# Banded attention and mixture of experts on one core: exponentials and last sums kept in PSUM, scaling on ScalarE, weight blocks stored by the queue of loads

## The chip, the core and the metric

The kernel runs on one core of a Trainium2 chip. The metric is the device time of one execution in microseconds (us). The kernel before takes 1236.85 us, the median of three runs (1235.83 to 1238.42). TensorE is written PE (its weight loads PEld), VectorE is DVE, ScalarE is ACT, GpSimd is POOL, and SyncE, which here only issues transfers, is SP.

## The reference

There are four batches, each of 8 heads, 768 positions and head size 64. For every query the scores over the keys get a slope times distance as bias; only the first `n_global` (8) keys and the last `n_local` (96) keys up to the query itself are kept. Then comes a softmax and the product with v:

```
a = exp(scores - max(scores)); a = a / (sum(a) + 1e-9); attn = a @ v
x = attn with the heads side by side        # 3072 rows x 512
p = domain_probs / (domain_probs.sum(-1) + 1e-9)
for e in 4 experts:                          # w1: 512 x 1024, w2: 1024 x 512
    out += p[:, e] * (relu(x @ w1[e]) @ w2[e])
```

All inputs and outputs are fp32.

## The kernel before

**Order of the work.** The attention of batch 0 runs alone ("first attention"). Then each batch's mixture of experts runs with the attention of the next batch spread between its products; batch 3's mixture runs alone. Up to a point shortly after the first attention every engine follows the program's order (`Ordered.on`). After that a planner orders the instructions of each engine by its own costs, with the program's order as priority. Engines take their own instructions strictly in order.

**Attention.** A tile is 128 queries of two heads (a pair), so there are 24 tiles in a batch. `scores` writes the scores of both heads into one PSUM bank (`ps`). `softmax` works on two tiles at a time. For the newer tile DVE adds the bias, finds the extreme and writes the biased scores to an SBUF tile `pb` (this is the custom instruction in the profile), and ACT takes the exponential in place in `pb` and sums it into `zsum`. For the older tile DVE adds 1e-9 to `zsum`, takes the reciprocal and multiplies the two halves of `pb` by it. `turn` transposes `pb` through PE into a PSUM tile `pt`, which ACT copies to SBUF as `pT`, and `weigh` multiplies with v into `px`. The bank `ps` is free once the biased scores are in SBUF. The first attention has 3 `ps`, 4 `pt` and 1 `px` banks; the later ones have 2, 2 and 1, and 3 banks `pm` are left for the mixture.

**Mixture.** Each expert's hidden width is cut into four, so a batch has 16 units. A unit has two parts. `first` makes a quarter of x @ w1 by seven block products in the manner of Strassen and Winograd, each of them six matmuls of 384 columns into one `pm` bank: A11, S2, S1, S3, A12, S4, A22 in this order. Partial sums go through the SBUF tiles p1, u, vv and c22. The last four products finish one of the four blocks of the hidden layer each: DVE adds the product and a partial sum (`add`), ACT takes the relu into the upper part of h (`relu`), and DVE later forms the lower part of h as relu minus the upper part. That "late" instruction is put off to the next `add` or the next product of `second` (`work_late`). `second` makes six tiles of h @ w2, each six matmuls of 512 columns into one `pm` bank, which DVE multiplies by the expert's probability and adds to `acc`. The program runs first(i), second(i-1), first(i+1), and so on. The three `pm` banks are handed out in the order of the products, so a product needs the bank of the third product before it.

**Weights.** Every unit's blocks of w1 and w2 are built once, while batch 0 runs: SP loads the raw weights, POOL forms the block sums, ACT and POOL split them into two parts. `load_w1` and `load_w2` end with `keep`, a store of the finished block to DRAM issued from POOL. The later batches load the kept blocks through SP (`fetch`). There are two buffers for each of w1 and w2 blocks, so a unit's buffer is written again two units later.

All engine calls go through one helper, so nearly every instruction shows the line L42 in the profile, and the tiles' names tell them apart. In the trace the sums of the last four products are `c<-pm,vv`, `p<-pm,p`, `vv<-pm,vv` and `u<-pm,u`, the relus are ACT `h<-c`, `h<-p`, `h<-vv`, `h<-u`, and the late instructions are DVE `h<-c,h`, `h<-p,h`, `h<-vv,h`, `h<-u,h`.

Of the kernel before, what the change touches and what calls it, by code (L numbers as in the profile page):

```python
# [9 lines left out]
F32 = mybir.dt.float32  # L10
F32R = mybir.dt.float32r
# [7 lines left out]
P = 128  # L19
# [6 lines left out]
def f32(ap):  # L26
    return ap.bitcast(F32)
# [158 lines left out]
def attn_moe_kernel(ctx: ExitStack, tc, q, k, v, n_global, n_local, domain_probs, w1, w2, out):  # L186
# [88 lines left out]
    class Pools:  # L275


        def __init__(self, stack, name, st, kd, qd, nat, natv, pb, ps, pt):
            def sbuf(part, bufs):
                return stack.enter_context(tc.tile_pool(name=f"{name}_{part}", bufs=bufs))  # L280

            def psum(part, bufs):
                return stack.enter_context(tc.tile_pool(name=f"{name}_{part}", bufs=bufs, space=PSUM))

            self.st, self.natv = sbuf("st", st), sbuf("natv", natv)
            self.kd, self.qd, self.nat, self.vg = sbuf("kd", kd), sbuf("qd", qd), sbuf("nat", nat), sbuf("vg", kd)
            self.pb, self.pT, self.small = sbuf("pb", pb), sbuf("pT", 4), sbuf("small", pb)
            self.ps, self.pt, self.px = psum("ps", ps), psum("pt", pt), psum("px", 1)
# [113 lines left out]
    def softmax(A, new, old):  # L402


        if old:
            pb, zsum = old["pb"], old["zsum"]
        if new:
            t, pr, ps = new["t"], new["pr"], new["ps"]
            cols = slice(0, P) if t == 0 else slice(0, 2 * P)
            bcol = slice(2 * P, 3 * P) if t == 0 else slice(0, 2 * P)  # L410
            new["pcol"] = pcol = slice(P, 2 * P) if t == 0 else slice(0, 2 * P)
            nmax = A.small.tile([P, 2], F32, name="nmax")
            new["zsum"] = A.small.tile([P, 2], F32, name="zsum")
            new["pb"] = A.pb.tile([P, 2, 2 * P], F32, name="pb")
        for j in range(2):
            if new:
                ve.tensor_tensor_reduce(
                    new["pb"][:, j, pcol], ps[:, j, cols], nbias[:, 2 * pr + j, bcol],
                    1.0, 3.0e38, ALU.add, ALU.min, nmax[:, j : j + 1],
                )  # L420
                ac.activation(
                    new["pb"][:, j, pcol], new["pb"][:, j, pcol], AF.Exp, bias=nmax[:, j : j + 1], scale=-1.0,
                    accum_out=new["zsum"][:, j : j + 1],
                )
            if old:
                if j == 0:
                    ve.tensor_scalar_add(zsum, zsum, 1e-9)
                else:
                    ve.reciprocal(zsum, zsum)
        if old:  # L430
            for j in range(2):
                ve.tensor_scalar_mul(pb[:, j, old["pcol"]], pb[:, j, old["pcol"]], zsum[:, j : j + 1])

    def turn(A, tile_):

# [198 lines left out]


    dp = main.enter_context(tc.tile_pool(name="dp", bufs=1, space=bass.MemoryType.DRAM))
    kept = {}

    def keep(key, dst):
        kept[key] = dp.tile(list(dst.shape), F32R, name="kept_{}_{}_{}".format(*key))  # L640
        po.dma_start(f32(kept[key]), f32(dst))

    def fetch(name, key, shape, view):
        dst = wp.tile(shape, F32R, name=name)
# [3 lines left out]
    def load_w1(i, wait=0, lead=5, hold=2):  # L648


        if i >= len(units):
            return
        b, e, g = units[i]
        if b > 0:
            wts[(i, 1)] = fetch("w1s", (e, g, 1), [P, 2, 7, 2, P], lambda t: {
                name: t[:, :, n] for n, name in enumerate(("A11", "A12", "A22", "S1", "S2", "S3", "S4"))
            })
            return
        for _ in range(wait):
            yield 1  # L660
        raw = rp.tile([P, KT, 2 * P], F32, name="raw1")
        sy.dma_start(raw, w1[e, :, g * 2 * P : (g + 1) * 2 * P].rearrange("(a p) f -> p a f", p=P))
        for _ in range(lead):
            yield 1
        a11, a21 = raw[:, 0:2, :P], raw[:, 0:2, P:]
        a12, a22 = raw[:, 2:4, :P], raw[:, 2:4, P:]
        sums = rp.tile([P, 4, 2, P], F32, name="sums")
        s1, s2, s3, s4 = (sums[:, n] for n in range(4))
        po.tensor_add(s1, a21, a22)
        po.tensor_sub(s2, s1, a11)  # L670
        po.tensor_sub(s3, a11, a21)
        po.tensor_sub(s4, a12, s2)
        for _ in range(hold):
            yield 1
        dst = wp.tile([P, 2, 7, 2, P], F32R, name="w1s")
        wts[(i, 1)] = {name: dst[:, :, n] for n, name in enumerate(("A11", "A12", "A22", "S1", "S2", "S3", "S4"))}
        for sl, src in (
            (slice(0, 2), raw[:, :, :P].rearrange("p (n a) f -> p n a f", n=2)),
            (slice(2, 3), a22.rearrange("p (n a) f -> p n a f", n=1)),
            (slice(3, 5), sums[:, 0:2]),  # L680
            (slice(5, 7), sums[:, 2:4]),
        ):
            ac.copy(dst[:, 0, sl], src)
            po.tensor_tensor(dst[:, 1, sl], src, f32(dst[:, 0, sl]), op=ALU.subtract)
            yield 1
        keep((e, g, 1), dst)

    def load_w2(i, lead=7):

# [12 lines left out]
        for f in range(2):  # L702
            ac.copy(dst[:, 0, f], raw[:, f])
            po.tensor_tensor(dst[:, 1, f], raw[:, f], f32(dst[:, 0, f]), op=ALU.subtract)
            yield 1
        keep((e, g, 2), dst)

    hs = {}

# [20 lines left out]
    def first(i):  # L730
# [9 lines left out]
        def add(out, pm, other):  # L740
            ve.tensor_add(out, pm[:, :HALF], other)
            work_late()

        p1, u, vv, c22 = (up.tile([P, HALF], F32, name=n) for n in ("p1", "u", "vv", "c22"))
        pm = product(i, "A11", "B11")
        ac.copy(p1, pm[:, :HALF])
        yield
# [2 lines left out]
        add(vv, product(i, "S1", "T1"), u)  # L750
        yield
        pm = product(i, "S3", "T3")
        add(c22, pm, vv)
        add(u, pm, u)
        relu(1, 1, c22)
        yield
        add(p1, product(i, "A12", "B21"), p1)
        relu(0, 0, p1)
        yield
        add(vv, product(i, "S4", "B22"), vv)  # L760
        relu(0, 1, vv)
        yield
        add(u, product(i, "A22", "T4"), u)
        relu(1, 0, u)
        yield

    accs = {}
# [1 line left out]
    def second(i):  # L769

        b, e, g = units[i]
        w2s, h = wts[(i, 2)], hs[i]
        for t in range(NQT):
            pm = ps_mm.tile([P, 512], F32, name="pm")
# [28 lines left out]
    bp = main.enter_context(tc.tile_pool(name="bp", bufs=1))  # L803
    Ordered.on = True
    with ExitStack() as start_stack:
        A = Pools(start_stack, "start", st=1, kd=2, qd=1, nat=2, natv=3, pb=4, ps=3, pt=4)
        for n, _ in enumerate(attention(0, A, early=True)):
            if n == 9:
                chores += [load_w1(0, lead=2), load_w2(0, lead=3)]
            if n == 18:  # L810
                chores.append(load_w1(1, lead=2, hold=3))
            if n == 2 * NQT + 5:
                chores.append(blocks(0, (0,), po))
            work_chores()
        mix = mixture()
        next(mix)
# [2 lines left out]
    up = main.enter_context(tc.tile_pool(name="up", bufs=1))  # L819
    op = main.enter_context(tc.tile_pool(name="op", bufs=1))  # L820
    ps_mm = main.enter_context(tc.tile_pool(name="ps_mm", bufs=3, space=PSUM))
    A = Pools(main, "att", st=1, kd=1, qd=1, nat=1, natv=1, pb=2, ps=2, pt=2)

# [76 lines left out]
```

## Time and profile before

| | us |
|---|---|
| median of three runs | 1236.85 |
| the profiled execution, device time | 1238.11 |
| its span, first to last instruction | 1236.3 |
| PE busy / weight loads | 1184.1 / 1055.6 |
| DVE busy | 922.9 |
| ACT busy | 429.7 |
| POOL busy | 241.2 |
| mean granted TensorE clock, as a share of full speed | 0.989 |

An engine's busy time is a sum over stages of different kinds: the first attention (to about 82 us), batch 0's mixture with batch 1's attention and the building of the weights (to about 372 us), two like stages without the building (to about 668 and 967 us), and batch 3's mixture alone. A row of the trace gives the start in us, the duration in us, the engine, what it writes and reads, the shape, the count where like rows are merged, and in brackets the idle time before it with what ended it.

### The profile page before, as it was taken

How to read it: one execution, taken by the hardware profiler on the slowest of the kernel's cores; microseconds unless marked ns; L12 is line 12 of the kernel's file. 1: busy time of each engine (PE TensorE's matmuls, PEld its weight loads, DVE VectorE, ACT ScalarE, POOL GpSimd, SP SyncE). 2: the span in 40 equal slices, each digit the busy share in tenths (PEclk: the TensorE clock that was granted, in tenths of full speed). 3: DMA queues.
4: the chain of work that ended last, by engine and by line, in shares of the span. 5: the costliest groups of instructions: out<-in, count | busy, mean ns of one | idle time of the engine just before them, and what ended most of it. 6: DMA issues, size and time to landing. Idle time of an engine off the chain costs nothing.

```text
span 1236.3 us, 18009 instructions
## 1 busy us (share of the span) xinstructions
PE 1184.1 (96%) x6624; PEld 1055.6 (85%) x6624; DVE 922.9 (75%) x2018; ACT 429.7 (35%) x1044; POOL 241.2 (20%) x258
## 2 busy tenths in 40 slices
PE   6779999999999999999999999999999999999998
PEld 4558898888888898898987898899898899999996
DVE  6878989877868777777767776867776866666665
ACT  4764454545442333333323233333332211111110
POOL 5576657466541000000002000000000100000000
PEclk9989999999999999999999999999999999999999
DMA  6557868786856666576655765757554555555532
GB/s 160 156 158 249 286 212 278 239 282 230 295 183 210 228 197 207 189 228 194 222 169 176 263 195 193 232 166 248 191 170 179 181 213 187 188 187 187 187 128 88
DMA packets 122704, 251.39 MB, mean 203 GB/s; under 512 B 83184, under 2 KB 91376, under 8 KB 106224
## 3 DMA queue, kind: packets, MB, share of 16 engines
q1 hardware_dynamic: 114256, 197.73, 50.5%
q0 software_dynamic: 4608, 46.14, 9.2%
q10 hardware_dynamic: 3744, 6.30, 1.4%
q8 instruction: 54, 0.88, 0.3%
q14 instruction: 42, 0.34, 0.1%
HBM read 174.11 MB, written 52.43 MB: 183 GB/s over the span
## 4 chain that ended last, share of the span: by engine, by line
PE 81%; DVE 9%; DMA 5%; ACT 2%; issue 1%; SPq 1%; POOL 1%; ACTq 0%; DVEq 0%; POOLq 0%
PE pm L42 71%; DMA qd<-st_q 5%; PE pt L42 4%; PE px L42 3%; PE ps L42 3%; DVE pb L42 3%; DVE h L42 1%; SPq L42 1%; DVE x L42 1%; ACT pb L42 1%; DVE zsum L42 1%; DVE u L42 1%; DVE xT L42 0%; DVE acc L42 0%; DVE vv L42 0%
## 5 line engine op out<-in xcount | busy, mean ns | idle before, releaser
L42 PE MATMUL pm<-w2s,h 128*128 128x512 f32 x2304 | 558.5, 396 | 9.5 <-DVE acc L42 9.1
L42 PEld LDWEIGHTS pm<-w2s,h 128*128 128x128 f32 x2304 | 429.1, 189 | 101.3 <-DVE acc L42 12.3
L42 DVE SCALAR_TENSOR_TENSOR acc<-pm,prob,acc 128x512 f32<-128x512 f32 x360 | 267.4, 748 | 120.9 <-PE pm L42 119.1
L42 PE MATMUL pm<-xT,w1s 128*128 128x384 f32 x1536 | 298.4, 339 | 4.9 <-ACT xT L42 3.0
L42 PEld LDWEIGHTS pm<-xT,w1s 128*128 128x128 f32 x1536 | 268.3, 189 | 8.2 <-ACT xT L42 3.4
L42 PE MATMUL pm<-xB,w1s 128*128 128x384 f32 x1152 | 229.1, 340 | 2.2 <-DVE vv L42 1.3
L42 PEld LDWEIGHTS pm<-xB,w1s 128*128 128x128 f32 x1152 | 202.5, 189 | 8.1 <-DVE vv L42 1.6
L42 ACT ACTIVATE pb<-pb,nmax 128x256 f32<-128x256 f32 (+1 forms) x192 | 93.1, 486 | 121.3 <-DVE nmax L42 114.2
L42 POOL COPY vg<-v 32x768 f32<-32x768 f32 x16 | 13.3, 829 | 525.7 <-DMA v<-in_v_dram 515.2
L42 ACT COPY p<-pm 128x384 f32<-128x384 f32 x64 | 30.6, 477 | 214.0 <-PE pm L42 213.9
L42 DVE TENSOR_SCALAR pb<-pb,zsum 128x256 f32<-128x256 f32 (+1 forms) x192 | 84.9, 474 | 2.8
L42 DVE TENSOR_TENSOR u<-pm,p 128x384 f32<-128x384 f32 x64 | 35.6, 556 | 61.1 <-PE pm L42 57.5
L42 DVE CUSTOM_DVE_ANT_0 pb<-ps,nbias 128x256 f32<-128x256 f32 (+1 forms) x192 | 71.9, 395 | 10.9 <-PE ps L42 7.1
L42 ACT ACTIVATE h<-c 128x384 fp32r<-128x384 f32 x64 | 33.6, 525 | 131.8 <-DVE c L42 131.8
L42 ACT COPY pT<-pt 128x512 f32<-128x512 f32 (+1 forms) x96 | 52.2, 544 | 76.0 <-PE pt L42 75.7
L42 DVE TENSOR_TENSOR u<-pm,u 128x384 f32<-128x384 f32 x128 | 70.5, 551 | 3.3 <-PE pm L42 2.6
L42 PE MATMUL pt<-ident,pb 128*128 128x128 f32 x352 | 57.2, 280 | 13.6 <-DVE pb L42 13.0
L42 PEld LDWEIGHTS pt<-ident,pb 128*128 128x128 f32 x352 | 43.3, 143 | 22.6 <-DVE pb L42 6.3
L42 PE MATMUL ps<-kd,qd 128*128 128x256 f32 x288 | 48.6, 283 | 6.0 <-DMA qd<-st_q 6.0
L42 PEld LDWEIGHTS ps<-kd,qd 128*128 128x128 f32 x288 | 44.5, 188 | 11.2 <-issue 7.2
L42 DVE TENSOR_TENSOR c<-pm,vv 128x384 f32<-128x384 f32 x64 | 35.6, 556 | 22.4 <-PE pm L42 21.7
L42 DVE TENSOR_TENSOR vv<-pm,u 128x384 f32<-128x384 f32 x64 | 35.6, 556 | 21.7 <-PE pm L42 21.0
(89 smaller groups left out, 1117.6 us busy)
## 6 DMA issues: line engine op xcount, KB each, us to landing
w1s<-kept SPq DMA_DIRECT2D x48, 1792.0 KB, 7.4
w2s<-kept SPq DMA_DIRECT2D x48, 1024.0 KB, 5.0
kept<-w1s POOLq DMA_DIRECT2D x16, 1792.0 KB, 6.6
qd<-st_q SPq DMA_DIRECT2D x96, 192.0 KB, 6.2
raw<-in_moe_w_dram SPq DMA_DIRECT2D x32, 512.0 KB, 4.4
kept<-w2s POOLq DMA_DIRECT2D x16, 1024.0 KB, 6.6
v<-in_v_dram SPq DMA_DIRECT2D x16, 384.0 KB, 4.2
out_dram<-acc ACTq DMA_DIRECT2D x24, 256.0 KB, 3.0
```

What stands on the lines that cost most here:

```text
L42: ins = fn(*args, **kwargs)
```

## The change

Four things change. In the first attention the biased scores and the exponentials stay in the `ps` bank, and only the scaling by DVE writes `pb`; there are 4 `ps` and 3 `pt` banks in place of 3 and 4. In the later attentions the addition of 1e-9 to `zsum` and the two scalings of a tile go from DVE to ACT (`Copy` with a bias or a scale); the reciprocal stays on DVE. In `first`, the last sum of each of the last four products is written back into the product's own `pm` bank, and relu and late instruction read it there; c22 is gone, and u takes the S3 product before c22's sum overwrites it. The stores of the built blocks are issued from SP at the beginning of the unit's `first` (w1) or `second` (w2).

```diff
-        def __init__(self, stack, name, st, kd, qd, nat, natv, pb, ps, pt):
+        def __init__(self, stack, name, st, kd, qd, nat, natv, pb, ps, pt, early):
+            self.early = early
...
+                e = new.setdefault("exp", {})[j] = ps[:, j, cols] if A.early else new["pb"][:, j, pcol]
                 ve.tensor_tensor_reduce(
-                    new["pb"][:, j, pcol], ps[:, j, cols], nbias[:, 2 * pr + j, bcol],
-                    1.0, 3.0e38, ALU.add, ALU.min, nmax[:, j : j + 1],
+                    e, ps[:, j, cols], nbias[:, 2 * pr + j, bcol], 1.0, 3.0e38, ALU.add, ALU.min, nmax[:, j : j + 1]
                 )
                 ac.activation(
-                    new["pb"][:, j, pcol], new["pb"][:, j, pcol], AF.Exp, bias=nmax[:, j : j + 1], scale=-1.0,
-                    accum_out=new["zsum"][:, j : j + 1],
+                    e, e, AF.Exp, bias=nmax[:, j : j + 1], scale=-1.0, accum_out=new["zsum"][:, j : j + 1]
                 )
             if old:
-                if j == 0:
+                if j == 1:
+                    ve.reciprocal(zsum, zsum)
+                elif A.early:
                     ve.tensor_scalar_add(zsum, zsum, 1e-9)
                 else:
-                    ve.reciprocal(zsum, zsum)
+                    ac.activation(zsum, zsum, AF.Copy, bias=1e-9)
         if old:
             for j in range(2):
-                ve.tensor_scalar_mul(pb[:, j, old["pcol"]], pb[:, j, old["pcol"]], zsum[:, j : j + 1])
+                if A.early:
+                    ve.tensor_scalar_mul(pb[:, j, old["pcol"]], old["exp"][j], zsum[:, j : j + 1])
+                else:
+                    ac.activation(pb[:, j, old["pcol"]], old["exp"][j], AF.Copy, scale=zsum[:, j : j + 1])
...
-    def keep(key, dst):
-        kept[key] = dp.tile(list(dst.shape), F32R, name="kept_{}_{}_{}".format(*key))
-        po.dma_start(f32(kept[key]), f32(dst))
+    def keep(i, n):
+        if (i, n) in waiting:
+            key, dst = waiting.pop((i, n))
+            kept[key] = dp.tile(list(dst.shape), F32R, name="kept_{}_{}_{}".format(*key))
+            sy.dma_start(f32(kept[key]), f32(dst))
...
-        keep((e, g, 1), dst)
+        waiting[(i, 1)] = (e, g, 1), dst
...
-        keep((e, g, 2), dst)
+        waiting[(i, 2)] = (e, g, 2), dst
...
-        p1, u, vv, c22 = (up.tile([P, HALF], F32, name=n) for n in ("p1", "u", "vv", "c22"))
+        def last(pm, other):
+            add(pm[:, :HALF], pm, other)
+            return pm[:, :HALF]
+
+        p1, u, vv = (up.tile([P, HALF], F32, name=n) for n in ("p1", "u", "vv"))
+        keep(i, 1)
...
         pm = product(i, "S3", "T3")
-        add(c22, pm, vv)
         add(u, pm, u)
-        relu(1, 1, c22)
+        relu(1, 1, last(pm, vv))
         yield
-        add(p1, product(i, "A12", "B21"), p1)
-        relu(0, 0, p1)
+        relu(0, 0, last(product(i, "A12", "B21"), p1))
         yield
-        add(vv, product(i, "S4", "B22"), vv)
-        relu(0, 1, vv)
+        relu(0, 1, last(product(i, "S4", "B22"), vv))
         yield
-        add(u, product(i, "A22", "T4"), u)
-        relu(1, 0, u)
+        relu(1, 0, last(product(i, "A22", "T4"), u))
...
         b, e, g = units[i]
+        keep(i, 2)
...
-        A = Pools(start_stack, "start", st=1, kd=2, qd=1, nat=2, natv=3, pb=4, ps=3, pt=4)
+        A = Pools(start_stack, "start", st=1, kd=2, qd=1, nat=2, natv=3, pb=4, ps=4, pt=3, early=True)
...
-    A = Pools(main, "att", st=1, kd=1, qd=1, nat=1, natv=1, pb=2, ps=2, pt=2)
+    A = Pools(main, "att", st=1, kd=1, qd=1, nat=1, natv=1, pb=2, ps=2, pt=2, early=False)
```

## Rows read from the trace of the kernel before

**Rows 1.** The page's first part: busy time, share of the span and instructions of the engines.

```profile
PE 1184.1 (96%) x6624; PEld 1055.6 (85%) x6624; DVE 922.9 (75%) x2018; ACT 429.7 (35%) x1044; POOL 241.2 (20%) x258
```

**Rows 2.** The busy times by stretch: from and to, its length, each engine's busy us (instructions), the granted clock, the transfers' share and GB/s. The stretches are the first attention, the passage to the mixture, batch 0 with the building of the weights, batch 1, batch 2, batch 3.

```profile
8.00:82.00 74.00, 56.21 (x407) 44.08 (x407) 60.98 (x221) 50.77 (x154) 39.59 (x47) 0.95 0.51 143
82.00:110.00 28.00, 22.45 (x98) 19.89 (x99) 22.77 (x38) 12.03 (x27) 18.74 (x21) 0.82 0.79 263
110.00:372.00 262.00, 255.71 (x1481) 228.59 (x1481) 217.18 (x455) 125.15 (x298) 154.98 (x161) 1.00 0.74 251
372.00:668.00 296.00, 291.39 (x1662) 261.99 (x1661) 219.18 (x502) 98.28 (x242) 9.78 (x8) 0.99 0.63 203
668.00:967.00 299.00, 294.60 (x1673) 263.88 (x1671) 223.98 (x506) 98.75 (x242) 12.20 (x8) 0.99 0.62 202
967.00:1236.30 269.30, 262.19 (x1302) 236.16 (x1302) 175.30 (x289) 42.99 (x82) 0.00 (x0) 0.99 0.47 171
```

**Rows 3.** The waits of PE over the whole span: who waited for whom, us in total, times, the longest.

```profile
PE pt L42 <- DVE pb L42: 13.0, 16, 1.9
PE pm L42 <- DVE acc L42: 9.1, 6, 2.0
PE ps L42 <- DMA qd<-st_q: 6.0, 8, 2.0
```

**Rows 4.** The timeline in one unit of batch 3, from the end of the product S3 (c takes it) to the weights and matmuls of A22 (`pm<-xT,w1s`, six).

```profile
1055.65 0.56 DVE L42 TENSOR_TENSOR c<-pm,vv 128x384 f32<-128x384 f32 x1 [0.48 <-PE pm L42]
1056.12 0.55 DVE L42 TENSOR_TENSOR u<-pm,u 128x384 f32<-128x384 f32 x1
1056.24 0.53 ACT L42 ACTIVATE h<-c 128x384 fp32r<-128x384 f32 x1 [3.18 <-DVE c L42]
1056.69 0.56 DVE L42 TENSOR_TENSOR p<-pm,p 128x384 f32<-128x384 f32 x1
1057.16 0.55 DVE L42 SCALAR_TENSOR_TENSOR h<-c,h 128x384 fp32r<-128x384 f32 x1
...
1057.36 1.05 PEld L42 LDWEIGHTS pm<-xT,w1s 128*128 128x128 f32 x6
1057.53 1.20 PE L42 MATMUL pm<-xT,w1s 128*128 128x384 f32 x6
```

**Rows 5.** The timeline of batch 3: c and the first weights of A22 behind it, in the first and the last of its 16 units.

```profile
986.34 0.56 DVE L42 TENSOR_TENSOR c<-pm,vv 128x384 f32<-128x384 f32 x1 [0.48 <-PE pm L42]
...
988.05 0.19 PEld L42 LDWEIGHTS pm<-xT,w1s 128*128 128x128 f32 x1
...
1210.72 0.56 DVE L42 TENSOR_TENSOR c<-pm,vv 128x384 f32<-128x384 f32 x1 [0.48 <-PE pm L42]
...
1212.43 0.19 PEld L42 LDWEIGHTS pm<-xT,w1s 128*128 128x128 f32 x1
```

**Rows 6.** The same two rows in the first and the last of the 32 units whose c lies in batches 1 and 2.

```profile
397.06 0.56 DVE L42 TENSOR_TENSOR c<-pm,vv 128x384 f32<-128x384 f32 x1 [0.48 <-PE pm L42]
...
399.14 0.19 PEld L42 LDWEIGHTS pm<-xT,w1s 128*128 128x128 f32 x1
...
959.06 0.55 DVE L42 TENSOR_TENSOR c<-pm,vv 128x384 f32<-128x384 f32 x1
...
960.13 0.19 PEld L42 LDWEIGHTS pm<-xT,w1s 128*128 128x128 f32 x1
```

**Rows 7.** The timeline at 104 us: a product of six matmuls that PE began only when DVE let it (matmuls and first weights both start at 104.25).

```profile
104.25 1.32 PE L42 MATMUL pm<-xB,w1s 128*128 128x384 f32 x6 [1.33 <-DVE vv L42]
```

**Rows 8.** DVE's groups from 0 to 92 us, by shape: busy us, mean ns of one, idle time before.

```profile
L42 DVE TENSOR_SCALAR pb<-pb,zsum 128x256 f32<-128x256 f32 x40 | 19.2, 521 | 0.7
L42 DVE CUSTOM_DVE_ANT_0 pb<-ps,nbias 128x256 f32<-128x256 f32 x40 | 16.6, 415 | 0.1
...
L42 DVE TENSOR_SCALAR pb<-pb,zsum 128x128 f32<-128x128 f32 x8 | 4.6, 610 | 0.1
...
L42 DVE CUSTOM_DVE_ANT_0 pb<-ps,nbias 128x128 f32<-128x128 f32 x8 | 2.2, 285 | 1.4 <-PE ps L42 1.4
```

**Rows 9.** ACT's groups by shape: the exponential from 400 to 700 us, then a relu (it reads SBUF) and a copy out of PSUM, both from 1000 to 1200 us.

```profile
L42 ACT ACTIVATE pb<-pb,nmax 128x256 f32<-128x256 f32 x40 | 20.1, 505 | 21.1 <-DVE nmax L42 21.1
...
L42 ACT ACTIVATE h<-c 128x384 fp32r<-128x384 f32 x13 | 6.8, 526 | 41.3 <-DVE c L42 41.3
...
L42 ACT COPY p<-pm 128x384 f32<-128x384 f32 x13 | 6.2, 480 | 106.7 <-PE pm L42 106.7
```

**Rows 10.** DVE's groups by shape: three from 92 to 372 us, the scaling again from 400 to 700 us, and a late instruction from 1000 to 1200 us.

```profile
L42 DVE TENSOR_SCALAR pb<-pb,zsum 128x256 f32<-128x256 f32 x40 | 28.2, 731 | 0.5
...
L42 DVE SCALAR_TENSOR_TENSOR h<-u,h 128x384 fp32r<-128x384 f32 x15 | 13.7, 912 | 0.7 <-ACT h L42 0.6
L42 DVE TENSOR_SCALAR zsum<-zsum 128x2 f32<-128x2 f32 x24 | 10.7, 444 | 2.7 <-ACT pb L42 2.7
...
L42 DVE TENSOR_SCALAR pb<-pb,zsum 128x256 f32<-128x256 f32 x40 | 12.9, 350 | 0.5
...
L42 DVE SCALAR_TENSOR_TENSOR h<-c,h 128x384 fp32r<-128x384 f32 x13 | 7.1, 548 | 0.0
```

**Rows 11.** The transfers from the scaled queries' staging (`qd<-st_q`, issued from SP) to landing, shortest, median and longest us: first from 92 to 372 us, then from 372 to 668 us.

```profile
DMA to landing us min/median/max: 2.5/5.8/9.0
...
DMA to landing us min/median/max: 2.5/6.8/11.2
```

More of the change, by code (lines that the diff above doesn't have):

```diff
@@ L636, in attn_moe_kernel @@
     dp = main.enter_context(tc.tile_pool(name="dp", bufs=1, space=bass.MemoryType.DRAM))
-    kept = {}
-    def keep(key, dst):
-        kept[key] = dp.tile(list(dst.shape), F32R, name="kept_{}_{}_{}".format(*key))
-        po.dma_start(f32(kept[key]), f32(dst))
+    kept, waiting = {}, {}
+    def keep(i, n):
[3 more added lines that the diff above has]
+            sy.dma_start(f32(kept[key]), f32(dst))
     def fetch(name, key, shape, view):
```

## The prediction

> **What bounds the kernel now.** I read the page's first part, then the table by stretch, then PE's waits, then the timeline of single units, and last the groups by shape where an edit needs a price.
>
> PE is busy 1184.1 of 1236.3 us [rows 1]. The stretches say where the missing 52 us are [rows 2]: 17.8 us in the first attention (56.2 of 74), 5.5 us in the passage, 6.3, 4.6 and 4.4 us in batches 0, 1 and 2, and 7.1 us in batch 3; the rest lies before 8 us. So from 110 us on PE sets the time. Whatever makes PE wait there is paid in full, and whatever frees another engine can return at most those few us. Only the first attention is different: DVE is busy 82% of it (60.98 of 74), ACT 69%, and PE's longest wait of the whole run is there, transposes for DVE's scaled exponentials, 13.0 us [rows 3].
>
> **Last sums in PSUM.** This is the edit that puts something in PE's way. A product needs the bank of the third product before it. A22 needs S3's. Before, S3's bank was free once c and u had read it; now it is held until S3's late instruction has read it. The chain in a unit of batch 3 [rows 4], counted from the start of DVE's first instruction on S3 (1055.65): u goes first, the last sum starts 0.47 later (the spacing of c and u) and takes 0.56, so it ends at 1.03. ACT follows 0.03 later, as it does on c (1056.21 to 1056.24). The relu now reads PSUM; the nearest row is the copy out of PSUM, 0.48 [rows 9], against 0.526 out of SBUF: 1.54. DVE follows 0.03 later for the late instruction, 0.55: 2.12. PE gets the bank 0.03 later: 2.15. Before, the weights of A22 were loaded at 1057.36, that is at 1.71. The lack is 0.44 us. A product that starts out of such a wait runs 1.32 us from its first weights [rows 7]; without one it runs 1.37 (1057.36 to 1057.53 + 1.20), so 0.05 comes back and PE loses 0.39 us. DVE is not the cause: the late instruction ended at 2.06 before, but nobody waited for it. No engine's order can mend it, because u must read S3 before the last sum overwrites it and each step needs the one before.
>
> All 16 units of batch 3 have the same distance, 1.71 from c to A22's weights, first and last alike [rows 5], and there is nothing else PE could do there: 16 x 0.39 = 6.2 us. The next products have a little air: second's first tile needs A12's bank, free at about 3.1 by the same steps, and would load weights at 1.71 + 0.44 + 1.04 = 3.2. I cost those at nothing; they have no more than 0.1 us of cover.
>
> In batches 0 to 2 attention work lies between some of the products. I took the same two rows in all 48 units there (in batches 1 and 2 from 2.08 behind c in the first to 1.07 in the last [rows 6]) and asked where 2.15, or the end of today's late instruction if later, comes after A22's weights. It does in about half of the units, and the positive lacks sum to about 5 us in each batch. What stands behind the waiting weights on PE is second's matmuls and the attention's. The planner may pull attention matmuls into such a gap, as it has in the other half; then the lack costs nothing. On the other side a tile's softmax between the steps makes them later. Bounds: 0, and 0.39 in every one of 48 units, 19 us. I take 10: about two thirds of the 15 found.
>
> Below nothing, this edit can gain only on DVE and ACT: 0.046 us per relu, which PE does not wait for.
>
> **Exponentials in PSUM in the first attention.** The scaling took 521 ns (40 of 128x256) and 610 ns (8 of 128x128) [rows 8]. With a PSUM source the nearest rows are the custom instructions that read the same bank, 415 and 285 ns: 40 x 0.106 + 8 x 0.325 = 6.8 us less on DVE. Half as many elements took longer, so part of the 521 is waiting rather than work: the same scaling takes 350 ns later, when POOL is idle, and 731 ns in batch 0, when POOL is busy 155 of 262 us [rows 2, 10]. DVE is busy 82% of the stretch, so about 5.6 us should reach the end. The exponential reading PSUM saves 48 x 0.046 = 2.2 us on ACT, hidden since ACT is only 69% busy. No row shows DVE or ACT writing PSUM; by the 0.046 us which separates the two memories for ACT's reads I bound it at 2.2 us either way. The bank `ps` is now held until the scaling, but with four banks `scores` needs the bank whose tile `turn` has already transposed on the same PE queue, so no wait is added. One `pt` fewer makes PE wait for an ACT copy one allocation earlier; ACT has 31% free, so I cost that at 0.6. The term is -5, between -9 (all of both savings) and +3.
>
> The Trainium skill's page "GPSIMD Engine Reference", section "1. Specifications", says that POOL and DVE share SBUF interfaces and hinder each other when a DVE instruction is in a two-port mode or has two SBUF inputs. The 731 ns against 350 agree with it. By that rule the scaling out of PSUM waits for POOL no more, and the late instructions, which from now on have one SBUF input, do not either.
>
> **Scaling on ACT.** In batch 0 this takes 28.2 + 10.7 = 39 us (the large scalings and `zsum`) off DVE, and the late u instructions (912 ns against 548 where POOL is idle) may lose 15 x 0.36 = 5.5 us as well [rows 10]. But PE idles only 6.3 us there, part of it for DVE. I take -3, between 0 and -6. In batches 1 and 2 DVE gets about 13 us shorter each, where PE idles 4.6 and 4.4, mostly at the passage of batches: 0. ACT gets 48 scalings of about 505 ns a batch (the exponential, same shape and memory [rows 9]), some 24 us; its share goes from 33% to 41% in batch 1 [rows 2]. Behind them on ACT stand relus and copies out of `pt`, so a relu can be up to 1 us later; that is in the upper bound of the bank's term.
>
> **Stores on SP's queue.** POOL loses 32 issues; PE's waits name POOL nowhere among their largest [rows 3], so this gains nothing. SP gets them at a time when the block is already needed by PE, so the store waits for nothing; but the loads of raw weights and `qd<-st_q` now stand behind 1.8 MB in the same queue. Batch 1 shows that case, with block loads of this size in that queue: staging to landing is 6.8 us in the median and 11.2 at worst, against 5.8 and 9.0 in batch 0 [rows 11], and PE's waits for it are 6.0 us in the whole run. I take +1, between 0 and +6 (its whole present sum again).
>
> **Sum.** -5 - 3 + 10 + 6.2 + 1 = +9.2 us. The profiled execution took 1238.11 us, 1.26 above the median; 1238.11 + 9.2 - 1.26 = 1246.0 us.
>
> **Rivals.**
> - *DVE's relief outweighs the bank.* For it: DVE is the busiest engine beside PE in the first attention, and its stalls there are real. Then -8 there and -6 in batch 0, the planner fills the gaps of batches 0 to 2 (0), batch 3 pays its 6.2, the queue 0: -8, 1229 us. Against it: batch 3's loss cannot be filled, and ACT at 69% comes up next in the first attention. It decides when batches 0 to 2 lose less than about 2 us together and the first attention gives more than 5.
> - *The bank costs more.* Sums, relus and late instructions of three banks depend on each other, with ACT's scalings between: every unit of batches 0 to 2 loses 0.39 and about 0.2 more at second's first tiles, 28 in place of 10: 1264 us. For it: the air there is under 0.1 us. Against it: DVE has less to do.
> - *It evens out:* first attention and batch 0 give 10, bank and queue take about the same: 1237 us.
> - *The bank is not held as I think,* because sums and relus in PSUM are so much shorter that 2.15 falls to 1.71, 0.15 us in each of three steps. The rows give 0.05 for one of them. Then -8 + 1: 1230 us. This counts with the first rival. The skill's page "ScalarE: Activation LUTs", section "Step-by-step: what each stage is for", speaks for it when it calls PSUM ACT's faster destination, and against it by its caveat that TensorE must not need most of PSUM; here all eight banks are taken. No run here shows a write of ACT to PSUM.
>
> **How the numbers follow.** Forecast 0.55 (its own range 1240 to 1255), more expensive bank 0.13, a costlier queue beside the forecast 0.04, even 0.08, faster 0.20. Within 0.2% (2.5 us either way, about what a measurement of this kernel can tell from no change) lie the even case and a little of the forecast: 0.10. Faster 0.20, slower 0.70. The range that leaves out 2 in 10 runs from 1229 to 1262.
>
> **What would show it.** In batch 3 of the changed kernel: weights of A22 with idle time before them, released by a DVE late instruction `h<-pm,h`, about 0.4 us in each of 16 units, and some 275 us for the stretch instead of 269. In batches 1 and 2: PE waits for DVE's h in the waits table. In the first attention: scaling at about 415 ns and a stretch some 5 us shorter. I am wrong if A22's weights show no wait in batch 3, or if the stretch before 82 us shrinks by over 10 us.

## The result and the profile after

The changed kernel takes 1243.77 us (median of five runs, 1242.94 to 1247.04) against 1236.74 (five runs, 1234.34 to 1238.42): 1.0063 of the time before, interval 1.0045 to 1.0082. It is slower by 7 us where 9.2 were forecast. That closeness is partly luck, as the stretches show. The profiled execution is the slowest of the five, 1247.04 us, so its stretches sum to 9.0 us over the profiled run of before.

The page's first part, the answer to [rows 1]:

```profile
PE 1194.8 (96%) x6624; PEld 1055.7 (85%) x6624; DVE 838.4 (67%) x1802; ACT 492.3 (40%) x1260; POOL 215.7 (17%) x226
```

DVE has lost 84.5 us, ACT has gained 62.6, POOL has lost 25.5. The engine that sets the time is PE. Its busy time rose by 10.7 us with the same 6624 matmuls, so its idle time alone does not show the loss. Of this rise 8.1 us lie in the first attention (56.4 us for 409 matmuls before, 64.5 for as many after), where the granted TensorE clock fell from 0.96 of full speed to 0.87, and 2.8 in batch 3. Whether the clock also sets the time there is asked below.

The waits of PE over the whole span, the answer to [rows 3]:

```profile
PE pm L42 <- DVE h L42: 13.4, 27, 2.0
PE pt L42 <- DVE pb L42: 7.9, 7, 1.7
PE pt L42 <- ACT ps L42: 7.5, 5, 2.4
...
PE ps L42 <- DMA qd<-st_q: 1.1, 4, 0.4
```

Two lines are new. Matmuls of the mixture wait for late instructions (h), and transposes of the first attention wait behind ACT's exponentials in `ps`. The waits for acc (9.1 us before) are gone, and those for the scaled queries' copies fell from 6.0 to 1.1.

To say where the time went, I cut each profiled run at events that every kernel has: the end of the first attention's last `px` matmul; DVE's first instruction on S3 in unit 0, in unit 15 and in unit 47 (so batch 0, and batches 1 and 2); and PE's end.

| stretch, us | before | after | difference |
|---|---|---|---|
| first attention, to the last px | 79.9 | 90.6 | +10.7 |
| passage, to unit 0's S3 | 12.7 | 8.4 | -4.3 |
| batch 0, units 0 to 15 | 277.5 | 276.0 | -1.5 |
| batches 1 and 2, units 15 to 47 | 589.0 | 587.4 | -1.6 |
| batch 3, unit 47 to PE's end | 271.1 | 276.8 | +5.7 |

The last line is as forecast. The first has the other sign.

**Batch 3.** The timeline of one unit of the changed kernel, the answer to [rows 4]. S3's sum is now `pm<-pm,vv`, behind u; the two relus on ACT are merged into one row.

```profile
1060.01 0.56 DVE L42 TENSOR_TENSOR u<-pm,u 128x384 f32<-128x384 f32 x1 [0.48 <-PE pm L42]
1060.49 0.56 DVE L42 TENSOR_TENSOR pm<-pm,vv 128x384 f32<-128x384 f32 x1
1061.05 0.57 DVE L42 TENSOR_TENSOR pm<-pm,p 128x384 f32<-128x384 f32 x1
1061.08 1.07 ACT L42 ACTIVATE h<-pm 128x384 fp32r<-128x384 f32 x2 [3.65 <-DVE pm L42]
1061.60 0.56 DVE L42 SCALAR_TENSOR_TENSOR h<-pm,h 128x384 fp32r<-128x384 f32 x1
...
1062.21 0.99 PEld L42 LDWEIGHTS pm<-xT,w1s 128*128 128x128 f32 x6 [0.47 <-DVE h L42]
1062.21 1.31 PE L42 MATMUL pm<-xT,w1s 128*128 128x384 f32 x6 [0.15 <-DVE h L42]
```

From u (1060.01) the last sum starts at +0.48, ACT follows at +1.07, the late instruction ends at +2.15, and A22's weights start at +2.20 where they stood at +1.71 before. The weights' row shows 0.47 of idle time with DVE's h as its releaser. The matmuls' row shows only 0.15, because the earlier product is still draining; a reader who looks at PE alone sees a third of the wait. From one unit's u to the next unit's it is 15.93 to 15.95 us, where c to c was 15.51 before.

**First attention.** The timeline of DVE in one tile of the changed kernel. The custom instruction is the biased sum of one head.

```profile
41.41 0.42 DVE L42 CUSTOM_DVE_ANT_0 ps<-ps,nbias 128x256 f32<-128x256 f32 x1
41.75 0.14 DVE L42 DVE_READ_ACCUMULATOR2_ANT nmax<- 128x1 f32 x1
41.75 0.17 DVE L42 TENSOR_SCALAR zsum<-zsum 128x2 f32<-128x2 f32 x1
42.53 0.43 DVE L42 CUSTOM_DVE_ANT_0 ps<-ps,nbias 128x256 f32<-128x256 f32 x1 [0.61 <-ACT ps L42]
42.88 0.14 DVE L42 DVE_READ_ACCUMULATOR2_ANT nmax<- 128x1 f32 x1
42.88 0.16 DVE L42 RECIPROCAL zsum<-zsum 128x2 f32<-128x2 f32 x1
43.08 0.88 DVE L42 TENSOR_SCALAR pb<-ps,zsum 128x256 f32<-128x256 f32 x2
```

The second head's sum waits 0.61 us for ACT. It shares nothing with ACT's exponential of the first head that it did not share before, except the bank: a tile of `ps` is 2 x 256 fp32, and both heads lie in one. While `pb` in SBUF took the sums, DVE only read that bank and ACT never touched it. Now each of them writes it, and the program lets them at it one after the other. (A tile of `ps` is exactly one bank, so no run here tells an order by tile from an order by bank.) The longest waits of DVE from 8 to 92 us in the changed kernel:

```profile
DVE ps L42 <- ACT ps L42: 12.2, 21, 0.7
DVE early_q L42 <- ACT early_q L42: 5.3, 7, 2.0
```

### The profile page after: what moved, and what is told of

Read it like the earlier page. It is cut to its first block, busy times and chain, and to the rows that moved or that the text cites. A ratio compares the mean times of both kernels' runs of the same rounds, so it can differ in the third digit from the quotient of the medians.

```text
span 1245.3 us, 17996 instructions
## 1 busy us (share of the span) xinstructions
PE 1194.8 (96%) x6624; PEld 1055.7 (85%) x6624; DVE 838.4 (67%) x1802; ACT 492.3 (40%) x1260; POOL 215.7 (17%) x226
## 4 chain that ended last, share of the span: by engine, by line
PE 80%; DVE 8%; DMA 4%; ACT 4%; POOL 3%; issue 1%; SPq 0%; ACTq 0%; POOLq 0%; DVEq 0%
PE pm L42 70%; PE pt L42 4%; PE px L42 3%; PE ps L42 3%; DMA qd<-st_q 2%; DVE pm L42 2%; ACT ps L42 1%; DVE h L42 1%; DMA raw<-in_moe_w_dram 1%; DVE ps L42 1%; POOL xB L42 1%; DVE u L42 1%; POOL sums L42 1%; DVE x L42 0%; POOL xT L42 0%
## 5 line engine op out<-in xcount | busy, mean ns | idle before, releaser
L42 PEld LDWEIGHTS pm<-xT,w1s 128*128 128x128 f32 x1536 | 264.2, 188 | 22.3 <-DVE h L42 17.1
L42 ACT ACTIVATE h<-pm 128x384 fp32r<-128x384 f32 x256 | 124.9, 491 | 209.9 <-DVE pm L42 206.0
L42 DVE SCALAR_TENSOR_TENSOR h<-pm,h 128x384 fp32r<-128x384 f32 x256 | 140.7, 553 | 18.6 <-ACT h L42 14.0
L42 ACT ACTIVATE pb<-pb,nmax 128x256 f32<-128x256 f32 (+1 forms) x144 | 70.0, 488 | 95.2 <-DVE nmax L42 94.9
L42 DVE TENSOR_TENSOR pm<-pm,vv 128x384 f32<-128x384 f32 x128 | 71.7, 560 | 2.1 <-PE pm L42 1.8
L42 ACT ACTIVATE pb<-pb,zsum 128x256 f32<-128x256 f32 (+1 forms) x144 | 62.8, 485 | 19.3 <-DVE zsum L42 19.3
L42 PEld LDWEIGHTS pt<-ident,pb 128*128 128x128 f32 x352 | 43.9, 143 | 27.6 <-ACT ps L42 12.2
L42 DVE CUSTOM_DVE_ANT_0 pb<-ps,nbias 128x256 f32<-128x256 f32 (+1 forms) x144 | 52.5, 396 | 9.5 <-PE ps L42 4.9
L42 DVE TENSOR_TENSOR u<-pm,u 128x384 f32<-128x384 f32 x64 | 35.7, 557 | 28.6 <-PE pm L42 28.2
L42 POOL TENSOR_TENSOR w2s<-raw,w2s 128x512 fp32r<-128x512 f32 x32 | 40.7, 1290 | 61.0 <-ACT w2s L42 60.9
```

Of the source, the lines that this page charges most:

```text
L42: ins = fn(*args, **kwargs)
```

## The experiments

**Each part alone.** Four kernels take one part of the change each, the rest being the kernel before.

The last sums in PSUM alone:

```diff
+        def last(pm, other):
+            add(pm[:, :HALF], pm, other)
+            return pm[:, :HALF]
...
-        add(c22, pm, vv)
         add(u, pm, u)
-        relu(1, 1, c22)
+        relu(1, 1, last(pm, vv))
...
-        add(p1, product(i, "A12", "B21"), p1)
-        relu(0, 0, p1)
+        relu(0, 0, last(product(i, "A12", "B21"), p1))
...
```

> Kernel before with the last sums in PSUM alone. Theory (A22 waits for S3's bank until S3's late instruction has read it): batch 3's units take 15.94 us each as in the changed kernel instead of 15.51, so batch 3 alone is 6.8 us longer, batches 0 to 2 together 0 to 10; the whole is slower by 7 to 14 us. Rival (the units of batch 3 are longer for another reason, such as the other order of transfers or ACT's new load): units stay at 15.51 and the whole stays within 2 us.

Measured: 1.0062 of the time before (1.0041 to 1.0083), 7.6 us. Units of batch 3 take 15.94 us, batch 3 is 276.9 against 271.1. Batch 0 is 3.2 us longer (280.7), batches 1 and 2 are 2.9 shorter (586.1). In the latter stretch nearly every kernel here comes out 2 to 6 us under the profiled run of before, those that change nothing in it too, so I read that as zero and not as a gain. The theory holds, the rival falls.

The sums also free DVE in batch 0. A late instruction now has one input in SBUF instead of two, and it no longer gets longer there while POOL works. The late instructions of batch 0 (shortest, median and longest ns; first and last start): of the four groups before the one that varied most, then all four together with the sums in PSUM.

```profile
L42 DVE SCALAR_TENSOR_TENSOR h<-u,h x15: 544/803/1637, 100.1 to 356.9; 128x384 fp32r<-128x384 f32 x15
...
L42 DVE SCALAR_TENSOR_TENSOR h<-pm,h x60: 540/548/559, 94.4 to 359.7; 128x384 fp32r<-128x384 f32 x60
```

The exponentials in PSUM alone, with 4 `ps` and 3 `pt` banks:

```diff
+                e = new.setdefault("exp", {})[j] = ps[:, j, cols] if A.early else new["pb"][:, j, pcol]
...
-        A = Pools(start_stack, "start", st=1, kd=2, qd=1, nat=2, natv=3, pb=4, ps=3, pt=4)
+        A = Pools(start_stack, "start", st=1, kd=2, qd=1, nat=2, natv=3, pb=4, ps=4, pt=3, early=True)
```

> Kernel before with the exponentials of the first attention in PSUM alone (4 ps and 3 pt banks). Theory (both heads of a tile lie in one bank, so DVE's second sum waits for ACT's first exponential): the first attention ends 8 to 12 us later than before, with some 10 us of DVE waiting for ACT, and the whole is slower by 5 to 11 us. Rival (the later end in the changed kernel comes from the other edits, the stores' queue above all): the first attention ends up to 5 us earlier, and the whole is faster by 2 to 6 us.

Measured: 1.0076 (1.0048 to 1.0104), 9.4 us by this ratio (the medians, 1246.46 and 1235.58, lie 10.9 apart). The first attention ends at 90.6, DVE waits 12.4 us for ACT, and no later stretch is longer than before by more than 0.1. This part alone costs more than the whole change.

The later scalings on ACT alone, and the stores on SP alone:

```diff
-                ve.tensor_scalar_mul(pb[:, j, old["pcol"]], pb[:, j, old["pcol"]], zsum[:, j : j + 1])
+                if A.early:
+                    ve.tensor_scalar_mul(pb[:, j, old["pcol"]], pb[:, j, old["pcol"]], zsum[:, j : j + 1])
+                else:
+                    ac.activation(pb[:, j, old["pcol"]], pb[:, j, old["pcol"]], AF.Copy, scale=zsum[:, j : j + 1])
```

```diff
-        po.dma_start(f32(kept[key]), f32(dst))
+            sy.dma_start(f32(kept[key]), f32(dst))
...
-        keep((e, g, 1), dst)
+        waiting[(i, 1)] = (e, g, 1), dst
```

> Kernel before with the later scalings on ACT alone. Theory (in batch 0 DVE is held up by POOL and loses 39 us of work): batch 0 is 2 to 5 us shorter, batches 1 and 2 stay within 1 us, the whole is faster by 2 to 5 us. Rival (ACT's queue delays the relus as much as DVE gains): within 2 us.

> Kernel before with the stores of the built blocks issued from SP at the unit's start, alone. Theory (POOL gets some 18 us of issue time back in and before batch 0, and the stores cost no wait): within 2 us, or faster by up to 3 in the passage behind the first attention. Rival (loads and the queries' copies stand behind 1.8 MB stores): slower by 2 to 6 us, with more waits of PE for the queries' copies in batch 0.

Measured: 1.0000 (0.9976 to 1.0025) and 0.9998 (0.9980 to 1.0015); neither moves the whole. The scaling's theory (2 to 5 us faster) falls. The stores do move time inside: the passage is 3.8 us shorter (8.9), batch 0 is 6.3 us longer (283.8).

The four parts sum to +1.4%, the whole change is +0.6%. So some of them must help each other. The next kernel tests one pair.

**Scaling and stores together.** Both diffs above at once, attention's beginning and the sums as before.

> Kernel before with the later scalings on ACT and the stores on SP, first attention and last sums as before. Theory (the stores shorten the passage behind the first attention by some 4 us, and alone they lose it again in batch 0, where DVE is held up by POOL; with the scalings off DVE that loss goes): passage some 4 us shorter, batch 0 no more than 1 us longer than before, the whole faster by 3 to 8 us. Rival (the stores' loss in batch 0 comes from their place in SP's queue, whatever DVE does): batch 0 again some 6 us longer, the whole within 2 us of before.

Measured: 0.9972 (0.9956 to 0.9987), 3.5 us faster by this ratio and 2.7 by the medians. The passage is 8.4 us, batch 0 is 279.1: 1.6 us longer than before instead of 6.3. A little over the 1 us that the theory allowed, but the rival's 6 us fall. Two rows show what happens in the passage, where the sums of x's blocks (`x<-x`) lead to the first product. DVE in the kernel before:

```profile
82.07 3.43 DVE L42 TENSOR_TENSOR x<-x 128x384 f32<-128x384 f32 x1
```

and in this kernel:

```profile
82.26 0.56 DVE L42 TENSOR_TENSOR x<-x 128x384 f32<-128x384 f32 x1
```

It is the same instruction, once 3.43 us and once 0.56. In the kernel before POOL runs four instructions in that time: the end of `xB` (82.04 to 83.05), two sums of raw weights (83.01, 1.39 in all) and a third (84.37, 0.71), and the store's issue stands right before (81.45). With the stores on SP the raw weights are loaded later, behind the stores, so POOL has nothing to do between 81.8 and 85.5. The Trainium skill's page "GPSIMD Engine Reference", section "1. Specifications", names DVE instructions with two SBUF inputs, as this one is, among those that contend with POOL; these rows agree. So the gain in the passage is not the issue time that POOL saves: it is building work moved out of the passage into batch 0. There it meets DVE's scalings out of SBUF (731 ns in batch 0 [rows 10]), and without these most of the loss is gone. That the whole 6.3 us were such contention is argued from this pair of runs, not shown row by row.

DVE's row accounts for about half of the gain in the passage. The rest lies between the product behind it and S3: in the kernel before POOL starts the `xT` that PE waits for only at 90.51, behind three more instructions on weights, and here at 85.46. In the kernel before:

```profile
90.51 1.30 POOL L42 TENSOR_TENSOR xT<-x,xT 128x384 fp32r<-128x384 f32 x1
...
91.87 0.69 PE L42 MATMUL pm<-xT,w1s 128*128 128x384 f32 x1 [0.80 <-POOL xT L42]
```

TensorE's clock explains at most a little of the gain. Behind an idle time of PE of 3.04 us the granted clock was 0.50 (1.2 GHz) from 86 to 92 us in the kernel before, and 1.00 (2.4 GHz) in the same stretch here. But with the stores alone it was 0.71 on average from 83.0 to 88.8, and the passage was 8.9 us there, half a microsecond longer than here.

This pair explains only some 3 us of the 9 or so by which the four parts exceed the whole. The stretches put the rest into batch 0: there the sums alone cost 3.2 us and this kernel 1.6, but the whole change, which has both, is 1.5 us shorter than before. In this kernel the late instructions still get long beside POOL:

```profile
L42 DVE SCALAR_TENSOR_TENSOR h<-c,h x15: 546/559/1690, 96.4 to 368.3; 128x384 fp32r<-128x384 f32 x15
```

In the changed kernel none takes over 560 ns. So the likely helper is the sums' relief of DVE, shown above; no run has sums, scaling and stores without the exponentials, so this stays argued.

**The first attention.** The changed kernel with both sums ahead of both exponentials:

```diff
+        if new and A.early:
+            for j in range(2):
+                e = new.setdefault("exp", {})[j] = ps[:, j, cols]
+                ve.tensor_tensor_reduce(...)
         for j in range(2):
             if new:
...
```

> Changed kernel with the order in the first attention's softmax changed: DVE's biased sums of both heads ahead of ACT's two exponentials. Theory (the two heads of a tile share one PSUM bank, so DVE's second sum waited for ACT's first exponential, and in this order it doesn't): DVE's waits for ACT's exponentials, 12 us in the changed kernel, go below 3 us, and the first attention ends 5 to 11 us earlier than at 90.6. Rival (the three pt banks hold PE up): the first attention still ends after 88 us and PE keeps waiting for pt.

Measured: 1.0066 (1.0040 to 1.0092) against the kernel before. The first attention ends at 86.5, 4.1 us earlier than in the changed kernel and under the 5 expected; DVE's wait for ACT's exponentials is gone from its list. But 6.6 of the 10.7 us stay. In this order ACT's first exponential must wait for the second sum, which writes the same bank, so the two engines still take turns. One tile shows it: the first sum has its extreme at 43.56, but ACT starts at 44.12, behind the second sum (43.59 to 44.02).

```profile
43.02 0.43 DVE L42 CUSTOM_DVE_ANT_0 ps<-ps,nbias 128x256 f32<-128x256 f32 x1
43.48 0.08 DVE L42 DVE_READ_ACCUMULATOR2_ANT nmax<- 128x1 f32 x1
43.59 0.43 DVE L42 CUSTOM_DVE_ANT_0 ps<-ps,nbias 128x256 f32<-128x256 f32 x1
...
44.12 0.45 ACT L42 ACTIVATE ps<-ps,nmax 128x256 f32<-128x256 f32 x1 [1.70 <-DVE zsum L42]
```

The banks alone (`ps=4, pt=3` in the kernel before):

> Kernel before with 4 ps and 3 pt banks in the first attention and nothing else. Theory (three pt banks are enough): the first attention ends within 1 us of 79.9. Rival (the pt bank taken away is what makes the changed kernel's first attention late): it ends 5 to 11 us later.

Measured in one run: 1234.65 us against 1234.56; the first attention ends at 79.6. Three `pt` banks cost nothing by themselves.

One head in PSUM, the other in SBUF, once each way:

```diff
-                e = new.setdefault("exp", {})[j] = ps[:, j, cols] if A.early else new["pb"][:, j, pcol]
+                e = new.setdefault("exp", {})[j] = ps[:, j, cols] if A.early and j == 1 else new["pb"][:, j, pcol]
```

> Kernel before with 4 ps and 3 pt banks, and only the second head's exponentials of the first attention in PSUM; the first head's stay in SBUF. Theory (DVE and ACT take turns on one bank): here ACT's first exponential works on SBUF while DVE writes the second sum to the bank, nobody waits for the other, and the first attention ends within 1.5 us of the kernel before (79.9). Rival (instructions that write PSUM, or a bank held until the scaling, make it late): it ends after 84 us.

> The mirror image: only the first head's exponentials in PSUM, the second head's in SBUF. Theory: DVE's second sum reads the bank in which ACT works on the first exponential, so DVE waits for ACT as in the changed kernel, some 10 us in all, and the first attention ends 5 to 11 us later than 79.9. Rival (writes to PSUM, or the held bank): the same end as with the second head in PSUM, since as many instructions write PSUM.

Measured in one run each, so without an interval: 1226.41 us and 1242.78 us (before 1234.8, its runs 1230.95 to 1241.24). The last instruction on the attention's output is ACT's copy `x<-px`; its row in the list of the tile `px` in the first 100 us gives the first and last start. In the kernel before, and then with the second head in PSUM:

```profile
L42 ACT COPY x<-px x8: 473/478/481, 26.0 to 79.9; 128x384 f32<-128x384 f32 x8
...
L42 ACT COPY x<-px x8: 478/482/540, 25.9 to 77.8; 128x384 f32<-128x384 f32 x8
```

and with the first head in PSUM:

```profile
L42 ACT COPY x<-px x8: 479/480/481, 29.7 to 89.5; 128x384 f32<-128x384 f32 x8
```

and DVE's first wait in that kernel:

```profile
DVE pb L42 <- ACT ps L42: 13.1, 22, 0.8
```

Both kernels write PSUM with the same instructions and hold the bank until the scaling, the faster one a little longer, since it scales the second head last; only who meets whom in the bank differs. With the second head there, DVE's list has no wait of a sum for ACT, and the first attention ends 2.1 us earlier than in the kernel before (77.8 against 79.9); with the first head there, the wait is back and it ends 9.5 later. This settles the cause: two engines at work in one bank. The direct cure, a bank for each head, was not tried.

The clock is not the cause either. From 8 to 77 us it was granted at 0.85 of full speed in the changed kernel and 0.96 before; but it was 0.94 with the second head in PSUM and 0.93 with the first, and their ends lie 11.6 us apart. The changed kernel ends only 1.2 us behind the latter, so little of the 10.7 us can be the clock's.

**The banks of the mixture.** The changed kernel with only S3's sum back in c22:

```diff
+        add(c22, pm, vv)
         add(u, pm, u)
-        relu(1, 1, last(pm, vv))
+        relu(1, 1, c22)
```

> Changed kernel with only the sum behind S3 back in SBUF (c22), the other three still in PSUM. Theory (A22 waits for S3's bank alone; the banks of A12, S4 and A22 come free in time): batch 3's units take 15.51 to 15.6 us, no idle time before A22's weights there, batch 3 some 6 us shorter than in the changed kernel, the whole 4 to 8 us faster than the changed kernel (so within 3 us of the kernel before). Rival (any late instruction on a bank holds PE up): second's first tiles wait instead, units stay at 15.8 to 15.95 us.

Measured: 1.0062 (1.0040 to 1.0084), no better than the changed kernel; units of batch 3 take 15.83 us. My theory falls and the rival holds. A22 no longer waits, but second's first tile does, for A12's bank. In batch 3 of this kernel:

```profile
1054.89 0.55 DVE L42 TENSOR_TENSOR u<-pm,u 128x384 f32<-128x384 f32 x1
...
1056.12 1.05 PEld L42 LDWEIGHTS pm<-xT,w1s 128*128 128x128 f32 x6
...
1056.97 0.55 DVE L42 SCALAR_TENSOR_TENSOR h<-pm,h 128x384 fp32r<-128x384 f32 x1
...
1057.57 0.53 PEld L42 LDWEIGHTS pm<-w2s,h 128*128 128x128 f32 x3 [0.39 <-DVE h L42]
```

A22's weights (1056.12) have no idle time; A12's late instruction ends at 1057.52, and second's weights start at 1057.57 after 0.39 of idle time. The tiles behind had air only because A22's wait gave it to them. So A12's bank has the same problem as S3's; whether the banks of S4 and A22 would come to have it was not tried.

The last sums in PSUM with four `pm` banks:

```diff
-    ps_mm = main.enter_context(tc.tile_pool(name="ps_mm", bufs=3, space=PSUM))
-    A = Pools(main, "att", st=1, kd=1, qd=1, nat=1, natv=1, pb=2, ps=2, pt=2)
+    ps_mm = main.enter_context(tc.tile_pool(name="ps_mm", bufs=4, space=PSUM))
+    A = Pools(main, "att", st=1, kd=1, qd=1, nat=1, natv=1, pb=2, ps=1, pt=2)
```

> Kernel before with the last sums in PSUM, and four pm banks in place of three (the later attentions give up one of their two ps banks). Theory (a product waits for the bank of the third product before it): with four banks A22 needs S1's bank, which is long free, and batch 3's units, where no attention runs, are back at 15.51 us. Batches 0 to 2 may take longer with one ps bank; that is not the question here. Rival (instructions on PSUM are slower or hinder PE): units stay at 15.9 us.

Measured in one run: 1220.17 us against 1234.8 (1230.95 to 1241.24). Units of batch 3 take 15.51 us. The timeline of one:

```profile
1192.74 0.56 DVE L42 TENSOR_TENSOR u<-pm,u 128x384 f32<-128x384 f32 x1 [0.48 <-PE pm L42]
...
1194.45 0.36 PEld L42 LDWEIGHTS pm<-xT,w1s 128*128 128x128 f32 x2
```

A22's weights stand at +1.71 again, without idle time. So the number of banks is the cause, and not the price of instructions on PSUM. That this kernel is also faster than the one before was not expected: batch 0 takes 273.1 us, batches 1 and 2 take 578.0, batch 3 takes 267.4, each less than before (277.5, 589.0, 271.1). PE's waits for acc at the ends of the batches (9.1 us before) are gone from its list here too. Whether four banks would do this with the sums in SBUF too, or only with the sums in PSUM, was not tried.

**A version that beats both.** Scaling on ACT, stores on SP, and only the second head's exponentials in PSUM:

> Kernel before with scaling on ACT, stores on SP, and only the second head's exponentials of the first attention in PSUM. Theory (no wait between DVE and ACT, and half of DVE's scalings out of POOL's way): the first attention ends at 78 to 80 us and the whole is 3 to 6 us faster than before, the same as scaling and stores alone or up to 2 us better. Rival: the first attention ends after 84 us, and the gain of scaling and stores is lost.

Measured: 1229.00 us, 0.9950 of the time before (0.9934 to 0.9966), 5.8 us. The first attention ends at 76.7, a little below the expected 78 to 80. It beats both kernels. Four `pm` banks on top of it were not tried.

## Why the prediction was right, and where not

**Last sums, batch 3: right.** Forecast 0.39 us per unit and 6.2 in all, measured 0.43 and 5.7 to 5.8. (16 times 0.43 is 6.9; the step from batch 2's last unit to batch 3's first, 27.29 us before and 26.12 after, gives 1.2 back.) The chain was forecast to reach PE at 2.15 behind u and did at 2.20: 0.02 more at the hand-over from DVE to PE, and 0.01 each for the last sum's start (0.48), the relu (0.49) and the late instruction (0.56). The releaser in the trace is the one named, and the four banks confirm it. So the rival with much shorter steps in PSUM falls.

**Air of the next products: wrong by a hair, and it mattered for the cure.** I cost them at nothing with 0.1 us of cover. In the changed kernel that held; with S3's sum back in SBUF the cover was gone and the wait moved one product on.

**Last sums, batches 0 to 2: oversized.** Forecast +10; alone this part costs 3.2 us in batch 0 and nothing that can be seen in batches 1 and 2. Up to unit 47's S3, PE's matmuls wait for h only nine times in the changed kernel, 8.5 us in all, where they waited 7.1 us for acc before. That the planner filled the other gaps, the case of the lower bound, is read from the missing loss and not from rows.

**First attention: wrong sign.** Forecast -5, between -9 and +3; measured +10.7, outside the bounds. The step that failed is "so no wait is added". I followed the bank as a thing that `scores` needs back, and found no wait there, rightly. I did not ask who else works in it: two engines on two halves of one bank. The Trainium skill's page "PSUM — Partial Sum Buffer", section "PSUM bank collisions raise a hardware error", says that two engines must be kept off one bank at the same time and that the guard belongs to the bank within a quarter of the partitions, not to the address (a tile here spans all four quarters); the 12.2 us of DVE's waits agree with it. Of the prices the exponential's was near (502 to 449 ns), the scaling's was not: 521 to 480, where 415 was forecast. The groups of the changed kernel's first 92 us:

```profile
L42 DVE TENSOR_SCALAR pb<-ps,zsum 128x256 f32<-128x256 f32 x40 | 17.5, 480 | 0.8
L42 DVE CUSTOM_DVE_ANT_0 ps<-ps,nbias 128x256 f32<-128x256 f32 x40 | 17.2, 429 | 10.6 <-ACT ps L42 10.4
...
L42 DVE TENSOR_SCALAR pb<-ps,zsum 128x128 f32<-128x128 f32 x8 | 2.4, 346 | 0.2
L42 DVE CUSTOM_DVE_ANT_0 ps<-ps,nbias 128x128 f32<-128x128 f32 x8 | 2.4, 297 | 3.3 <-ACT ps L42 1.8 <-PE ps L42 1.4
```

The scalings saved 3.9 us (19.9 against 23.8 [rows 8]) where 6.8 were forecast. The sums took 0.8 more, and the reads of their accumulator got longer too. In all, DVE's busy time up to the last `px` fell by 1.0 us only (62.95 to 61.93, 231 instructions in both), so the relief from which the forecast of -5 came was mis-sized even without the wait. A steady price took the place of a varying one: out of PSUM each of the 40 large scalings took 474 to 486 ns, out of SBUF 340 to 1359. And busy time says nothing of two engines that must take turns.

**Scaling on ACT: forecast -3, measured 0 alone.** Its worth appears only together with the stores.

**Stores: forecast +1 with "this gains nothing" for POOL, measured 0 alone.** The queue's cost did not come: PE's waits for the copies fell. What I missed is that a later store makes later loads, and so moves POOL's work out of the passage (-3.8) into batch 0 (+6.3).

**The sum.** +9.2 forecast, +7.0 measured by the medians. Two terms were wrong in opposite ways: the first attention by 15.7 us, and the passage with batches 0 to 2 by 15.4 (10 - 3 + 1 = +8 forecast, -7.4 in the profiled run, of which some 3 come from the profiled run of before being long in batches 1 and 2). Only batch 3 is as forecast. The direction rested on the bank's wait, which is real and costs 7.6 us alone; but the first attention's wait, which I did not see, costs 9.4 alone, and by the parts it would have made the kernel slower without the other.

## What to carry to other kernels

When data move into PSUM, ask of each bank both questions: until when is it held and which product needs it back, and which engines work in it at the same time, whatever halves they use. Count the banks in the rotation: with three, a chain of sum, relu and late instruction of 2.15 us held up a product that came 1.71 us later, and one bank more ended that. An edit that costs nothing alone may pay with another one: stores and scaling were worth 0 and 0 apart, and some 3 us together.

## What the runs showed of the hardware

Reading the accumulator behind DVE's sum takes 133 ns on average when the sum goes to PSUM, against 80 before; the sum itself takes 429 instead of 415. ACT's relu takes 491 ns out of PSUM against 526 out of SBUF, and its exponential 449 in and out of PSUM against 502. The same DVE instruction on two SBUF inputs took 0.56 us with POOL idle and 3.43 beside four POOL instructions. With one of its two inputs in PSUM a late instruction took 540 to 559 ns in all 60 cases of batch 0 (the sums alone in PSUM), with both in SBUF 541 to 1637 (the kernel before). The scaling of 128x256 took 474 to 486 ns out of PSUM and 340 to 1359 out of SBUF in the first attention. A wait of 0.47 us before a product's first weights shows as 0.15 before its matmuls.
